# Attention units 4 to 9 scored in pairs, and the layer-2 matmuls dealt out anew, in a fused window-attention and feed-forward kernel

## The chip, the cores and the metric

The kernel runs on one core of one Trainium2 chip. The metric is the device time of one execution in microseconds (us). Three runs of the kernel before took 279.0 to 279.9 us, with a median of 279.62. Everything below that is said of a single instruction comes from one further execution of that kernel, taken by the hardware profiler.

## What is computed

Eight batches, eight heads, 576 tokens each and a head size of 64: attention in a band of 32 keys to either side, then a feed-forward network with one hidden layer over all 4608 tokens.

```python
scores = scale * np.matmul(q, k.transpose(0, 1, 3, 2))
mask = np.abs(pos[:, None] - pos[None, :]) <= window      # window = 32
scores = np.where(mask, scores, -1000000000.0)
attn = np.exp(scores - np.max(scores, axis=-1, keepdims=True))
attn = attn / (np.sum(attn, axis=-1, keepdims=True) + 1e-09)
x = np.matmul(attn, v).transpose(0, 2, 1, 3).reshape(B * S, H * D)   # 4608 x 512
h = x @ w_in                                                          # 512 x 2048
out = (h * (1.0 / (1.0 + np.exp(-1.702 * h)))) @ w_out                # 2048 x 512
```

## The kernel before

**Units and tiles.** The 4608 tokens are 36 units of 128 queries, and nine tiles of four units (512 tokens). A unit goes through `scores` (line 267: 24 small matmuls for q times k, then two exponentials on ScalarE), `band` (line 308: one multiplication by the mask on VectorE), `values` (line 316: 32 small matmuls with v) and `norm` (line 335: reciprocal and multiplication on VectorE). `x_T` and `x_T2` turn the result so that the features lie on the partitions. The first four units are scored in pairs (`scores_pair`, line 286): one pair takes 40 matmuls, the mask being added on TensorE by `seed` (line 261) ahead of the scores.

**Feed-forward.** Layer 1 of a tile (`l1_group`, line 512, called for n = 0 to 3) and layer 2 of half a tile (a pair of unit rows; `layer2`, line 597) are each split in 2 x 2 blocks and computed with seven products instead of eight; P1, P7, P6, P2, P5 or P4, P3 are the products. Tile 0 has plain layer 1 (`layer1_plain`, line 477), interleaved by hand with the first attention units in `opening` (line 662).

**The list of layer 2.** `layer2_plain(0, 0)` gives 32 closures with one matmul each, `layer2` gives 56 for every pair: eight for each product, in the order

```python
ps = [pair(*x) for x in pairs[:-1]] + [pair(*pairs[-1], end=(self.nc.sync, dve))]
out = ps[0][1] + ps[0][7]
for x, y in zip(ps, ps[1:]):
    out += x[6] + x[2] + x[4] + x[5] + y[1] + x[3] + y[7]
```

They stand in one list, `self.l2` (called `more` in `run`). `do(l2, n)` takes the next n of it and issues them; so the order on TensorE is written by hand, as numbers in the calls of `do`: in `opening`, in `first_layer1` (line 958, layer 1 of tile 1: four numbers for every n, used after P1, P7, P2 and P4 of layer 1), in `run` (line 895) and, from the third tile on, in `front` (line 820) and `back` (line 847, with the table `SHARES`). The list never learns where it is cut: which layer-2 matmul meets which cut depends on the sum of all numbers before.

**The banks of layer 2.** A pair has two banks of PSUM, LA and LB, each with two halves of 256 columns: a and c in LA, b and e in LB. P1 sums into a, and P7 into c. With P7's eighth matmul `after(7)` (lines 610 to 615) issues two copies, on the engine `seed2` (ScalarE at first, VectorE from line 944 on):

```python
self.copy(self.seed2, st["b"], st["a"])       # seed: P1's sum into bank LB
self.copy(self.seed2, st["s7"], st["c"])
```

P6 then goes on summing in b, on top of the copy. All engines work through their own instructions in order.

**Loads.** GpSimd issues the transfers of q, k, v (with a change of type) and of the weights, at first all together in `opening`, later by `LOADS` and by `fetch` in `first_layer1`; it also copies v with an offset of 64 tokens (`odd_v`, line 218). SyncE issues the transposing transfers and the stores.

Of the kernel before, what the change touches and what calls it, by code (L numbers as in the profile page):

```python
# [15 lines left out]
F32 = mybir.dt.float32  # L16
# [6 lines left out]
SQ = 64  # L23
# [3 lines left out]
class _Kernel:  # L27
# [7 lines left out]
    def __init__(self, ctx, tc, q, k, v, w_in, w_out, out):  # L35
        self.tc, self.nc = tc, tc.nc
        self.q, self.k, self.v, self.w_in, self.w_out, self.out = q, k, v, w_in, w_out, out
        self.B, self.H, self.S, self.D = q.shape
        self.N = self.B * self.S
        self.DM = self.H * self.D  # L40
        self.DFF = w_in.shape[1]
        self.scale = 1.0 / (self.D ** 0.5)
        self.NU = self.N // 128
        self.NT = self.N // TILE

        def pool(name, bufs, **kw):
# [5 lines left out]
        self.stage, self.kT, self.qT = {}, {}, {}  # L52
        self.p, self.acc, self.x, self.xT, self.xs = {}, {}, {}, {}, {}
        self.g, self.gs, self.o, self.sc = {}, {}, {}, {}
# [102 lines left out]
    def kq_tile(self, t):  # L157

        if ("T", t) not in self.stage:
            s = self.sb("gs", [128, 4, 576 + TILE], BF16, 2, "kq4")  # L160
            k, q = self.stage["T", t] = s[:, :, 0:576], s[:, :, 576:]
            for i in range(4):
                self.kT[4 * t + i] = k[:, :, 128 * i:128 * i + 128]
                self.qT[4 * t + i] = q[:, :, 128 * i:128 * i + 128]
            self.kT[4 * t + 4] = k[:, :, 512:576]
        return self.stage["T", t]
# [41 lines left out]
    def load_v(self, u, which=slice(None)):  # L208
# [21 lines left out]

    def place(self, c, u):
        t = self.sb(c + "T", [128, 4, 128], BF16, 7)
        (self.kT if c == "k" else self.qT)[u] = t
        return t
# [31 lines left out]

    def scores(self, u, tag):
        kT, q = self.kT[u], self.qT[u]
        nxt = self.k_first if u == self.NU - 1 else self.kT[u + 1][:, :, 0:64]
        sc = self.score_banks(tag)  # L270
        for hp in range(4):
            c = 128 * hp
            start = hp == 0
            for eo in range(2):
                r = slice(64 * eo, 64 * eo + 64)
                lo, hi = sc[eo][0:64], sc[eo][64:128]
                self.mm(lo[:, c:c + 64], kT[r, hp, 0:64], q[r, hp, 0:64], start=start)
                self.mm(hi[:, c:c + 128], kT[r, hp, 64:128], q[r, hp, :], start=start)
# [4 lines left out]
        for eo in range(2):  # L283
            self.nc.scalar.activation(p[:, eo].rearrange("k h s -> k (h s)"), sc[eo], AF.Exp, scale=self.scale)  # L284

    def scores_pair(self, u):
# [16 lines left out]
        for x in range(2):  # L303
            for eo in range(2):
                self.nc.scalar.activation(p[:, eo, x].rearrange("k h b s -> k (h b s)"), sc[2 * x + eo], AF.Exp,
                                          scale=self.scale)

    def band(self, u, eng=None):
# [3 lines left out]
        pv = p.rearrange("p e (h b) s -> p (e h) b s", b=2)  # L312
        msk = self.mask[:, a:b + 1:b - a, :].rearrange("p (o b) s -> p o b s", o=1)
# [40 lines left out]
    def values_four(self, u):  # L354
# [5 lines left out]
        for tag in self.FOUR:  # L360
            lo, n, pad = self.four(tag)
            for i in range(n):
                x, h = divmod(lo + i, self.H)
                at, more = pad + i * (D + 1), pad * (i == 0)
                for blk in range(2):
                    vt = (self.ve[(u + x) % 9], self.odd(u + x))[blk].rearrange("p h d -> p (h d)")
                    self.mm(self.acc[u][tag][64 * blk:64 * blk + 64, at - more:at + D + 1],
                            p[x][:, h % 2, h // 2 * 2 + blk, :], vt[:, h * (D + 2) - more:h * (D + 2) + D + 1],
                            start=(i == 0))
# [106 lines left out]

    def layer1_plain(self, t, f, half, tag, later=None, kept=None):

# [11 lines left out]
        if kept is not None:  # L490
            self.nc.vector.tensor_copy(kept, h)
            h = kept
# [169 lines left out]
    def opening(self):  # L662
# [18 lines left out]
        self.load_w1(256, 256)  # L681
        self.load_w1(512)
        for u in (0, 1):
# [7 lines left out]
        self.load_v(4, slice(1, 2))  # L691
        for u in (5, 6, 7, 8):
            self.load_v(u)
        for c in range(4):
            self.load_w2(c)
# [3 lines left out]
        self.seed(0, "AC")  # L699
        self.scores_pair(0)  # L700
        self.T_first("k", 1, ("LA", "LB"), (dve, dve))
        self.T_first("q", 1, ("B", "E"), (dve, act))
# [40 lines left out]
        act.activation(self.spark, self.spark, AF.Exp)  # L743
        gelus = []
        kept = [self.sb("s7", [128, 512], F32, 2)]
        room = self.sb("xs", [128, 2, 512], F32, 1, "room")
        kept += [room[:, i, :] for i in range(2)]
        h[:], n[0] = ["LA"], 0
        l1(1, 10, later=gelus, kept=kept[0])
        for i in (3, 1):  # L750
            self.w1_sums((i,), 1)
        for u in (4, 5, 6, 7):
            self.odd_v(u, pool)
        self.load_kq("k", 8)
        for u in (8, 9, 10, 11):
            self.fetch(u)
        h[:], n[0] = ["LB", "LA"], 0
# [8 lines left out]
        self.band(5)  # L766
        self.norm(4)
        h[:], n[0] = ["B", "E"], 0
        l1(None, 14, later=gelus)
        self.band(6)  # L770
        l1(None, 15, later=gelus)
        self.values(5, "t")
        self.norm(5)
        self.band(7)
        self.values(6, "AC")
        self.do(self.l2, 6)
        self.do(gelus)
        self.norm(6)
        self.values(7, "t")
        self.norm(7)  # L780
        self.do(self.l2, 2)
        self.w1_sums((2,), 1)
        self.g0_sum(0)
        self.x_T2(4, "A", act)
        self.do(self.l2, 4)
# [109 lines left out]
    def run(self):  # L895
        pool, act = self.nc.gpsimd, self.nc.scalar
        self.l2eng = self.seed2 = act
        more = self.l2 = self.layer2_plain(0, 0) + self.layer2([(i, j) for i in range(self.NT) for j in range(2)][1:-1],
# [17 lines left out]
        do(more, 4)  # L916
        self.values(8, "t")
        self.values(9, "AC")
        self.odd_v(12, pool)
        self.odd_v(13, pool)  # L920
        self.scores(11, "BE")
        self.norm(8)
        self.band(10)
        self.norm(9)
        do(more, 8)
        self.scores(12, "t")
        do(more, 4)
        self.values(10, "AC")
        self.norm(10)
        self.band(11)  # L930
        self.scores(13, "BE")
        do(more, 8)
        self.x_T2(8, "t", act)
        self.values(11, "AC")
        self.norm(11)
        self.scores(14, "BE")
        do(more, 4)
        self.x_T(10, "A", dve)
        do(more, 2)
        self.x_T(11, "C", dve)  # L940
        self.scores(15, "t")
        do(more, 2)
        do(self.x_sums(2))
        self.seed2 = dve
        self.odd_v(14, pool)
        self.odd_v(15, pool)
        self.ahead("kq", 16)
        late = self.back(2)
# [9 lines left out]
    def first_layer1(self):  # L958
# [7 lines left out]
        for n in range(4):  # L966
# [3 lines left out]
            self.odd_v(8 + n, self.nc.gpsimd)  # L970
            self.fetch(12 + n)
# [7 lines left out]
            self.l1_group(1, n, fill, lambda i: self.do(dv, 1))  # L979
            dv += self.g_sums(1, 2 * n, 2) + extra[n]  # L980
# [47 lines left out]
```

## Time and profile before

| of the kernel before | |
|---|---|
| three runs, median (lowest to highest) | 279.62 us (279.0 to 279.9) |
| the profiled execution, its own time | 279.59 us |
| span of its instructions | 277.8 us |
| TensorE busy | 266.3 us of the span, 3652 matmuls |
| VectorE, ScalarE, GpSimd busy | 212.1, 197.3, 138.6 us |
| packets of the transfers | 37.74 MB |

In the profile PE is TensorE's matmuls, PEld its weight loads, DVE VectorE, ACT ScalarE, POOL GpSimd and SP SyncE. L70 is the line that issues every matmul, L67 the line that issues every copy, so that such groups are told apart by the names of what they write and read: `o<-b,g` writes the tile o and reads b and g. Starts are microseconds from the span's beginning. Matmuls overlap in their pipeline: each lasts longer than the distance to the next.

### The profile page before, as it was taken

How to read it: one execution, taken by the hardware profiler on the slowest of the kernel's cores; microseconds unless marked ns; L12 is line 12 of the kernel's file. 1: busy time of each engine (PE TensorE's matmuls, PEld its weight loads, DVE VectorE, ACT ScalarE, POOL GpSimd, SP SyncE). 2: the span in 40 equal slices, each digit the busy share in tenths (PEclk: the TensorE clock that was granted, in tenths of full speed). 3: DMA queues.
4: the chain of work that ended last, by engine and by line, in shares of the span. 5: the costliest groups of instructions: out<-in, count | busy, mean ns of one | idle time of the engine just before them, and what ended most of it. 6: DMA issues, size and time to landing. Idle time of an engine off the chain costs nothing.

```text
span 277.8 us, 8904 instructions
## 1 busy us (share of the span) xinstructions
PE 266.3 (96%) x3652; PEld 224.8 (81%) x3652; DVE 212.1 (76%) x487; ACT 197.3 (71%) x346; POOL 138.6 (50%) x216
## 2 busy tenths in 40 slices
PE   1989999999999999999999999999999999999994
PEld 1668656888888888888888888888888888888883
DVE  3455898897899788878888887888798878855631
ACT  2586896989896689568966895698569856577420
POOL 8895597999592089729641974294430000000000
PEclk9999999999999999999999999999999999999999
DMA  8999999999999999999999999999992024202033
GB/s 86 166 206 195 178 207 168 170 150 164 139 162 189 155 121 153 174 176 166 188 178 153 130 172 148 163 145 139 136 136 77 2 82 74 76 2 76 2 113 117
DMA packets 150809, 37.74 MB, mean 136 GB/s; under 512 B 138608, under 2 KB 146416, under 8 KB 150768
## 3 DMA queue, kind: packets, MB, share of 16 engines
q0 software_dynamic: 106656, 18.42, 96.4%
q1 hardware_dynamic: 43664, 18.23, 38.0%
q8 instruction: 28, 0.46, 0.7%
q10 hardware_dynamic: 448, 0.52, 0.6%
q14 instruction: 13, 0.11, 0.1%
HBM read 36.83 MB, written 9.44 MB: 167 GB/s over the span
## 4 chain that ended last, share of the span: by engine, by line
PE 91%; DVE 4%; ACT 2%; issue 1%; POOL 1%; POOLq 0%; DVEq 0%
PE o L70 40%; PE h L70 39%; PE sc L70 5%; PE pv L70 4%; PE tp L179 1%; PE tp L203 1%; POOL kq L154 1%; ACT p L284 1%; DVE xn L345 1%; PE tp L409 0%; PE tp L249 0%; DVE b L433 0%; DVE o_sb L67 0%; PE tp L397 0%; ACT kq L67 0%
## 5 line engine op out<-in xcount | busy, mean ns | idle before, releaser
L524 ACT ACTIVATE g<-h 128x512 f16<-128x512 f32 x128 | 72.2, 599 | 37.9 <-PE h L70 31.6
L70 PEld LDWEIGHTS <-g 128*128 128x128 f16 x568 | 54.6, 98 | 8.1
L70 PE MATMUL h<-xs,a 128*128 128x256 f16 x384 | 57.6, 272 | 0.3 <-DVE h L537 0.3
L70 PEld LDWEIGHTS <-a 128*128 128x128 f16 x512 | 49.7, 97 | 8.8 <-issue 0.6
L70 PEld LDWEIGHTS <-w 128*128 128x128 f16 x496 | 47.6, 98 | 7.7
L70 PE MATMUL h<-xT,w 128*128 128x256 f16 (+1 forms) x368 | 53.6, 277 | 0.1
L70 PE MATMUL o<-w,g 128*128 128x256 f16 (+1 forms) x304 | 49.8, 284 | 0.0
L70 PEld LDWEIGHTS <-gs 128*128 128x128 f16 x416 | 39.7, 98 | 5.5 <-issue 0.2
L227 POOL COPY vo<-ve 64x264 int32<-64x264 int32 x71 | 35.1, 494 | 16.4 <-DMA ve<-in_v_dram 10.0
L70 PE MATMUL o<-b,gs 128*128 128x256 f16 x280 | 43.3, 273 | 0.0
L70 PE MATMUL o<-b,g 128*128 128x256 f16 x264 | 38.5, 273 | 0.0
L213 POOL DMA_DIRECT2D ve<-in_v_dram x40 | 34.1, 860 | 5.4 <-DMA w<-in_moe_w_out_dram 1.8
L537 DVE TENSOR_TENSOR h<-h,s 128x512 f32<-128x512 f32 x32 | 22.3, 698 | 18.3 <-PE h L70 18.2
L284 ACT ACTIVATE p<-sc 128x512 bf16<-128x512 f32 x64 | 32.6, 619 | 1.1 <-PE sc L70 1.0
L143 POOL DMA_DIRECT2D qst<-in_q_dram x35 | 28.2, 807 | 1.7 <-issue 1.6
L543 DVE TENSOR_TENSOR h<-h,s 128x512 f32<-128x512 f32 x32 | 22.3, 698 | 7.6 <-PE h L70 7.4
L143 POOL DMA_DIRECT2D kst<-in_k_dram x31 | 26.4, 854 | 0.6 <-DMA qst<-in_q_dram 0.4
L67 ACT COPY h<-h 128x512 f32<-128x512 f32 x32 | 18.8, 589 | 10.4 <-PE h L70 9.8
L886 POOL COPY seen<-gs 1x1 f16<-1x1 f16 x17 | 3.3, 196 | 39.3 <-DVE gs L456 39.3
L314 DVE TENSOR_TENSOR p<-p,mask 128x1024 bf16<-128x1024 bf16 x32 | 21.8, 699 | 0.7 <-ACT p L284 0.7
L67 ACT COPY o_sb<-o 128x256 f32<-128x256 f32 (+1 forms) x24 | 11.1, 462 | 12.8 <-PE o L70 12.8
L67 ACT COPY s<-h 128x512 f32<-128x512 f32 x32 | 19.2, 600 | 0.8
(94 smaller groups left out, 377.8 us busy)
## 6 DMA issues: line engine op xcount, KB each, us to landing
out_dram<-o_sb SPq DMA_DIRECT2D x33, 256.0 KB, 3.8
ve<-in_v_dram POOLq DMA_DIRECT2D x32, 128.0 KB, 6.3
kst<-in_k_dram POOLq DMA_DIRECT2D x25, 128.0 KB, 6.0
qst<-in_q_dram POOLq DMA_DIRECT2D x21, 128.0 KB, 5.7
w<-in_moe_w_out_dram POOLq DMA_DIRECT2D x4, 512.0 KB, 11.1
w<-in_moe_w_in_dram POOLq DMA_DIRECT2D x3, 512.0 KB, 9.3
qst<-in_q_dram POOLq DMA_DIRECT2D x7, 96.0 KB, 6.0
kq<-in_q_dram POOLq DMA_DIRECT2D x2, 256.0 KB, 6.0
```

What stands on the lines that cost most here:

```text
L67: (eng.copy if eng is self.nc.scalar else eng.tensor_copy)(out, in_)
L70: self.nc.tensor.matmul(out, lhsT, rhs, start=start, stop=stop, skip_group_check=True)
L143: self.nc.gpsimd.dma_start(t[off:off + n], src[b, :, s:s + n, :].rearrange("h s d -> s h d"))
L154: self.nc.gpsimd.dma_start(self.stage["first"][0:n // j, :, at:at + j], src[0, :, lo:lo + n, :].rearrange("h (p j) d -> p h j d", j=j))
L213: self.nc.gpsimd.dma_start(t[off:off + n, :, :self.D], self.v[b, :, s:s + n, :].rearrange("h s d -> s h d"))
L227: eng.tensor_copy(*((words(vo[64:128]), words(self.ve[u % 9][64:128])), (words(vo[0:64]), words(nxt)))[i])
L284: self.nc.scalar.activation(p[:, eo].rearrange("k h s -> k (h s)"), sc[eo], AF.Exp, scale=self.scale)
L314: (eng or self.nc.vector).tensor_mul(pv, pv, msk.to_broadcast([128, 8, 2, SQ]))
L524: act.activation(g[:, f, 256 * half:256 * half + 256], bank.rearrange("p (i n) -> p i n", i=2), AF.Gelu_apprx_sigmoid)
L537: dve.tensor_add(e, b, s7)
L543: dve.tensor_add(c, b, s7)
L886: self.nc.gpsimd.tensor_copy(self.seen, self.gs[t - (n == 0)][0:1, 2, c, 255:256])
```

## The change

1. **Pairs.** Units 4 and 5, 6 and 7, 8 and 9, 12 and 13 are scored together by the new `scores_two`: 40 matmuls for two units in place of 48, into four banks, with four exponentials as before. `band_two` masks units 4 to 9 by halves of heads (two multiplications for two units, as before), with three masks that `setup_pairs` lays out ahead by 12 small copies on VectorE. For this q of units 8 and 9, and of 12 and 13, lies in one tile (`place`).
2. **Opening.** Layer 1 of blocks 8 to 11 of tile 0 is done with 16 matmuls of 512 columns in place of 32 of 256; sums are parked in three single tiles; the table of the exponential is called up one block earlier; the activations of the parked blocks come in another order.
3. **Loads.** The third transfer of w_in goes in halves. Values 8 come in two halves (`load_half`), the second after the copies of v for units 4 to 7. Values 13 to 16 are asked for in n = 3 of `first_layer1` only, and q and k of unit 16 earlier in `run`.
4. **Sums of `first_layer1`** (VectorE) are dealt out by a new table, `sums`.
5. **Numbers of `do`.** In `first_layer1` n = 0 takes 1, 2, 3, 3 in place of 1, 1, 3, 3. The calls in `run` are cut anew, 64 in all as before; `opening` takes 18 as before, and so does each later n what it took. Scores 8 to 10 stand after the first 8 of `run`, and the second exponential of unit 10 after another 20.
6. **Banks.** Values 11 go to bank t (one reciprocal and one multiplication in place of two and two), x of units 8 and 9 is turned in bank A, x of 10 and 11 in one go in bank C.

```diff
+    def load_half(self, u, at):
+        b, s = divmod(128 * u + at, self.S)
+        self.nc.gpsimd.dma_start(self.ve[u % 9][at:at + 64, :, :self.D],
+                                 self.v[b, :, s:s + 64, :].rearrange("h s d -> s h d"))
...
+    def scores_two(self, u, tags):
+        k, q = [self.kT[u + i] for i in range(3)], self.qT[u]
+        sc = [x for tag in tags for x in self.score_banks(tag)]
+        for hp in range(4):
+            c = 256 * (hp % 2)
+            for eo in range(2):
+                r = slice(64 * eo, 64 * eo + 64)
+                for i in range(5):
+                    lo, hi = max(0, 64 * (i - 1)), min(256, 64 * (i + 1))
+                    rows = slice(64 * (i % 2), 64 * (i % 2) + 64)
+                    self.mm(sc[2 * (hp // 2) + eo][rows, c + lo:c + hi], k[i // 2][r, hp, rows], q[r, hp, lo:hi],
+                            start=c == 0 and i < 2)
...
+    def band_two(self, u):
+        m = self.masks[u].rearrange("p (e y) n -> p e y n", e=1, y=1).to_broadcast([128, 2, 2, 4 * SQ])
+        for x in range(2):
+            p = self.pair[u][:, :, x].rearrange("k e (y b) s -> k e y (b s)", y=2)
+            self.nc.vector.tensor_mul(p, p, m)
+
+    def setup_pairs(self):
...
+        for u in (4, 6, 8):
...
+                    self.nc.vector.tensor_copy(m[:, 0, at:at + SQ], self.mask[:, x, :])
...
-        self.load_w1(512)
+        self.load_w1(512, 256)
+        self.load_w1(768, 256)
...
-        l1(0, 8)
+        l1(None, 8)
...
-        l1(0, 10)
-        l1(1, 8)
+        l1(None, 9)
...
+        l1(None, 10, later=gelus, kept=kept[0])
+        act.activation(self.spark, self.spark, AF.Exp)
...
-        l1(1, 10, later=gelus, kept=kept[0])
+        l1(None, 11, later=gelus, kept=kept[1])
...
-        self.scores(4, "AC")
-        self.scores(5, "t")
-        l1(None, 12, later=gelus, kept=kept[1])
-        self.scores(6, "BE")
-        self.band(4)
-        l1(None, 13, later=gelus, kept=kept[2])
-        self.scores(7, "AC")
+        self.scores_two(4, ("AC", "t"))
+        copies, first = [], []
+        l1(None, 12, later=gelus, kept=kept[2], when=copies)
+        h[:] = ["LB"]
+        self.scores_two(6, ("BE", "AC"))
+        self.band_two(4)
+        l1(None, 13, later=first)
...
@@ run
-        self.l2eng = self.seed2 = act
+        self.l2eng, self.seed2 = self.nc.vector, act
...
-        self.scores(8, "t")
-        self.scores(9, "AC")
+        do(more, 8)
+        self.scores_two(8, ("t", "AC"))
+        exps = self.scores(10, "BE", True)
...
-        do(more, 20)
-        self.scores(10, "BE")
-        do(more, 12)
-        self.l2eng = dve
-        self.band(8)
-        self.band(9)
         do(more, 4)
+        self.band_two(8)
+        self.l2eng = act
+        do(more, 16)
+        do(exps)
+        do(more, 8)
         self.values(8, "t")
...
@@ first_layer1
+            chunks = ((1, 2, 3, 3), (1, 1, 3, 5), (2, 2, 8, 4), (2, 2, 6, 6))[n]
+            sums = ((0, 0, 1, 1, 2), (3, 1, 0, 1, 3), (1, 0, 2, 1, 2), (2, 1, 1, 0, 1))[n]
             def fill(i):
-                self.do(self.l2, dict(zip((1, 7, 2, 4), ((1, 1, 3, 3), (1, 1, 3, 5), (2, 2, 8, 4), (2, 2, 6, 6))[n]))[i])
-                self.do(dv, {1: 2, 7: 1, 2: 0, 4: 2}[i] if n else {1: 0, 7: 1, 2: 0, 4: 1}[i])
+                at = (1, 7, 2, 4).index(i)
+                self.do(self.l2, chunks[at])
+                self.do(dv, {1: sums[0], 7: sums[1], 2: 0, 4: sums[4]}[i])
```

Where the new numbers leave the cuts is best seen in the order of the instructions. On TensorE, in `front` of the fourth tile, the kernel before had P7 of a pair (it reads b3 and g), then the scores of two units (they read qT and kT), then P6 (it reads b2 and gs):

```order
L70 LDWEIGHTS g_2351
L70 MATMUL o_2742<-b3_78,g_2351 128x256
L70 LDWEIGHTS kT_2349
L70 MATMUL sc_2854<-qT_2435,kT_2349 64x64
L70 LDWEIGHTS kT_2349
L70 MATMUL sc_2854<-qT_2435,kT_2349 64x128
...
L70 LDWEIGHTS kT_2441
L70 MATMUL sc_2883<-qT_2439,kT_2441 64x64
L70 LDWEIGHTS gs_2422
L70 MATMUL o_2845<-b2_77,gs_2422 128x256
```

At the same place the changed kernel has:

```order
L71 LDWEIGHTS g_2315
L71 MATMUL o_2705<-b3_78,g_2315 128x256
L71 LDWEIGHTS gs_2386
L71 MATMUL o_2808<-b2_77,gs_2386 128x256
L71 LDWEIGHTS kT_2313
L71 MATMUL sc_2818<-qT_2399,kT_2313 64x64
L71 LDWEIGHTS kT_2313
L71 MATMUL sc_2818<-qT_2399,kT_2313 64x128
```

P6's first matmul has moved ahead of the 48 score matmuls, to the place right behind P7's eighth. The VectorE instructions there keep their order (the copy that seeds b is `o_2845<-o_2742` before and `o_2808<-o_2705` now):

```order
L67 COPY o_sb_2509<-o_2507 128x512
L67 COPY o_2845<-o_2742 128x256
L67 COPY s7o_2846<-o_2742 128x256
L455 TENSOR_TENSOR gs_2422<-gs_2422,g_2351 128x512
L456 TENSOR_TENSOR gs_2422<-g_2351,gs_2422 128x512
```

```order
L68 COPY o_sb_2472<-o_2470 128x512
L68 COPY o_2808<-o_2705 128x256
L68 COPY s7o_2809<-o_2705 128x256
L509 TENSOR_TENSOR gs_2386<-gs_2386,g_2315 128x512
L510 TENSOR_TENSOR gs_2386<-g_2315,gs_2386 128x512
```

Nothing moved on that engine. The second place is TensorE in `first_layer1` with n = 2, at the first pair of the list: before, eight matmuls of layer 1 (they write h) stood between P7 (`b3_78,gs_608`) and P6 (`b2_77,gs_608`):

```order
L70 LDWEIGHTS gs_608
L70 MATMUL o_1129<-b3_78,gs_608 128x256
L70 LDWEIGHTS a1_72
L70 MATMUL h_1151<-xs_983,a1_72 128x256
...
L70 LDWEIGHTS w1_70
L70 MATMUL h_1152<-xs_983,w1_70 128x256
L70 LDWEIGHTS gs_608
L70 MATMUL o_1209<-b2_77,gs_608 128x256
```

Now:

```order
L71 LDWEIGHTS gs_620
L71 MATMUL o_1112<-b3_78,gs_620 128x256
L71 LDWEIGHTS gs_620
L71 MATMUL o_1190<-b2_77,gs_620 128x256
L71 LDWEIGHTS a1_72
L71 MATMUL h_1135<-xs_969,a1_72 128x256
```

Again P6's first matmul follows P7's eighth, and the matmuls of layer 1 follow it. The third place is ScalarE in `run`, at the second pair, which still has its seed copied there (`o_1475<-o_1416` before, `o_1451<-o_1420` now; p is what an exponential writes):

```order
L67 COPY o_sb_1211<-o_1209 128x512
L67 COPY o_1475<-o_1416 128x256
L67 COPY s7o_1476<-o_1416 128x256
L284 ACTIVATE p_1451<-sc_1519 128x512
L284 ACTIVATE p_1451<-sc_1520 128x512
```

```order
L68 COPY o_sb_1192<-o_1190 128x512
L293 ACTIVATE p_1402<-sc_1377 128x512
L68 COPY o_1451<-o_1420 128x256
L68 COPY s7o_1452<-o_1420 128x256
L293 ACTIVATE p_1402<-sc_1500 128x512
```

One exponential, the one held back of unit 10, now stands between the store's copy and the seed. Over the whole list, P6's first matmul stands directly behind P7's eighth of the same pair at 15 places of 17 in the changed kernel and at none in the kernel before; at the two others, in the closing run of layer 2, matmuls of the other of the last two pairs lie between them in both kernels.

More of the change, by code (lines that the diff above doesn't have):

```diff
@@ L52, in __init__ @@
         self.stage, self.kT, self.qT = {}, {}, {}
+        self.pair = {}
         self.p, self.acc, self.x, self.xT, self.xs = {}, {}, {}, {}, {}
@@ L265, in seed, with scores @@
             self.mm(x, self.ident, self.bias, start=True)
-    def scores(self, u, tag):
+    def scores(self, u, tag, hold=False):
         kT, q = self.kT[u], self.qT[u]
@@ L306, in scores_pair @@
                                           scale=self.scale)
+    def scores_two(self, u, tags):
[10 more added lines that the diff above has]
+                            start=c == 0 and i < 2)
+        self.pp = self.sb("p", [128, 2, 2, 8, SQ], BF16, 2)
+        self.pair[u] = self.pp
+        p = self.pp.rearrange("k e x (y b) s -> k e x y b s", y=2)
+        for i in range(2):
+            self.p[u + i] = p[:, :, :, :, 2 * i:2 * i + 2, :]
+        for x in range(2):
+            for eo in range(2):
+                self.nc.scalar.activation(p[:, eo, x].rearrange("k y b s -> k (y b s)"), sc[2 * x + eo], AF.Exp,
+                                          scale=self.scale)
+    def band_two(self, u):
+        m = self.masks[u].rearrange("p (e y) n -> p e y n", e=1, y=1).to_broadcast([128, 2, 2, 4 * SQ])
+        for x in range(2):
+            p = self.pair[u][:, :, x].rearrange("k e (y b) s -> k e y (b s)", y=2)
+            self.nc.vector.tensor_mul(p, p, m)
+    def setup_pairs(self):
+        self.masks = {}
+        for u in (4, 6, 8):
+            m = self.cst.tile([128, 1, 4 * SQ], BF16, name=f"mask{u}")
+            self.masks[u] = m
+            for i in range(2):
+                cross = [(2 * (u + i) + j) % 9 == 8 for j in range(2)]
+                for j, x in enumerate((0 if cross[0] else 1, 2 if cross[1] else 3)):
+                    at = SQ * (2 * i + j)
+                    self.nc.vector.tensor_copy(m[:, 0, at:at + SQ], self.mask[:, x, :])
     def band(self, u, eng=None):
@@ L475, in g_tile, with layer1_plain @@
         return self.g[t]
-    def layer1_plain(self, t, f, half, tag, later=None, kept=None):
+    def layer1_plain(self, t, f, half, tag, later=None, kept=None, when=None):
         g = self.g_tile(t)
@@ L490, in layer1_plain @@
         if kept is not None:
-            self.nc.vector.tensor_copy(kept, h)
+            do = lambda h=h: self.nc.vector.tensor_copy(kept, h)
+            do() if when is None else when.append(do)
             h = kept
@@ L691, in opening @@
         self.load_v(4, slice(1, 2))
-        for u in (5, 6, 7, 8):
+        for u in (5, 6, 7):
             self.load_v(u)
+        self.load_half(8, 0)
         for c in range(4):
@@ L739, in opening @@
         self.g0_sum(7)
-        l1(0, 10)
-        l1(1, 8)
-        self.T_four("q", "tA", (dve, act))
[L743 to L747, printed above, removed]
+        l1(None, 9)
+        gelus = []
+        kept = [self.sb("s7", [128, 512], F32, 2) for i in range(2)]
+        kept.append(self.sb("xs", [128, 512], F32, 1, "room"))
+        l1(None, 10, later=gelus, kept=kept[0])
+        act.activation(self.spark, self.spark, AF.Exp)
+        self.T_four("q", "tA", (dve, act))
         h[:], n[0] = ["LA"], 0
-        l1(1, 10, later=gelus, kept=kept[0])
+        l1(None, 11, later=gelus, kept=kept[1])
         for i in (3, 1):
@@ L920, in run @@
         self.odd_v(13, pool)
+        self.ahead("kq", 16)
         self.scores(11, "BE")
@@ L924, in run @@
         self.norm(9)
-        do(more, 8)
-        self.scores(12, "t")
-        do(more, 4)
+        do(more, 12)
+        self.scores_two(12, ("t", "BE"))
         self.values(10, "AC")
+        self.band(11)
         self.norm(10)
[L930 to L934, printed above, removed]
+        do(more, 6)
+        self.values(11, "t")
         self.norm(11)
         self.scores(14, "BE")
+        self.x_T2(8, "A", act)
         do(more, 4)
-        self.x_T(10, "A", dve)
-        do(more, 2)
-        self.x_T(11, "C", dve)
+        self.x_T2(10, "C", dve)
         self.scores(15, "t")
-        do(more, 2)
+        do(more, 6)
         do(self.x_sums(2))
-        self.seed2 = dve
+        self.seed2 = self.l2eng = dve
         self.odd_v(14, pool)
         self.odd_v(15, pool)
-        self.ahead("kq", 16)
         late = self.back(2)
```

38 lines of the change are left out of this document (24 added, 14 removed).

## The prediction

> **What bounds the kernel now.** I read the page first: busy shares, the slices, and the shares of the chain that ended last.
>
> ```profile
> PE 266.3 (96%) x3652; PEld 224.8 (81%) x3652; DVE 212.1 (76%) x487; ACT 197.3 (71%) x346; POOL 138.6 (50%) x216
> PE   1989999999999999999999999999999999999994
> PEclk9999999999999999999999999999999999999999
> PE 91%; DVE 4%; ACT 2%; issue 1%; POOL 1%; POOLq 0%; DVEq 0%
> ```
>
> TensorE is busy for 266.3 of 277.8 us, at an undivided clock in all 40 slices, and it makes up 91% of the chain. Then I took stretches of the steady part, where one tile takes 27.4 us; the columns after the stretch's length are the busy time of PE, PEld, DVE, ACT and POOL, then the clock.
>
> ```profile
> 99.60:127.00 27.40, 27.40 (x385) 23.90 (x384) 23.17 (x54) 20.78 (x37) 19.18 (x32) 1.00 2.23 163
> 127.00:154.40 27.40, 27.40 (x385) 23.90 (x384) 23.05 (x54) 20.78 (x37) 15.41 (x26) 1.00 1.68 166
> 181.80:209.20 27.40, 27.40 (x386) 23.89 (x384) 23.06 (x53) 20.78 (x37) 14.66 (x27) 1.00 1.36 134
> ```
>
> TensorE does not stop at all there. So whatever holds it up is paid in full, and taking work off another engine brings nothing. Last I read the waits, and the durations of the two kinds of instruction that the change brings together.
>
> ```profile
> DVE o L67 <- PE o L70: 4.5, 12, 1.5
> PE h L70 <- DVE h L537: 0.3, 1, 0.3
> L70 PE MATMUL o<-b,g 128*128 128x256 f16 x264 | 38.5, 273 | 0.0
> L67 DVE COPY o<-o 128x256 f32<-128x256 f32 x15 | 6.5, 433 | 4.6 <-PE o L70 4.5
> L67 ACT COPY o<-o 128x256 f32<-128x256 f32 x2 | 0.8, 388 | 0.0
> ```
>
> The seed copy (`o<-o`) waits for TensorE 12 times; the other direction, P6 waiting for the seed copy, does not occur in the list of waits at all. That is the state that the change touches.
>
> **The large term: P6 right behind P7.** The seed copy starts when P7's eighth matmul is through, and P6's first matmul sums on top of it. The timeline of one place, in `front`:
>
> ```profile
> 128.97 1.04 PE L70 MATMUL o<-b,g 128*128 128x256 f16 x8
> 129.17 0.69 DVE L67 COPY o_sb<-o 128x512 f32<-128x512 f32 x1 [0.52 <-PE o L70]
> 129.94 0.70 PE L70 MATMUL sc<-qT,kT 64*64 64x64 bf16 x48
> 130.04 0.43 DVE L67 COPY o<-o 128x256 f32<-128x256 f32 x1 [0.18 <-PE o L70]
> 130.57 1.05 PE L70 MATMUL o<-b,gs 128*128 128x256 f16 x8
> ```
>
> P7's eight end at 128.97 + 1.04 = 130.01, the copy starts at 130.04 and ends at 130.47, P6 starts at 130.57. The 48 score matmuls between fill the copy's time almost to the point. P7's spacing is (1.04 - 0.273)/7 = 0.11 us, so its eighth starts at 129.74, and the next matmul could start at 129.85. In the changed kernel that next one is P6, which cannot start before the copy's end plus the way from VectorE to TensorE. For that way there is one row, the only matmul that waits for VectorE in the list above:
>
> ```profile
> 56.63 1.04 PE L70 MATMUL o<-b,gs 128*128 128x256 f16 x8
> 57.18 0.69 DVE L537 TENSOR_TENSOR h<-h,s 128x512 f32<-128x512 f32 x1
> 57.88 0.42 ACT L67 COPY o<-o 128x256 f32<-128x256 f32 x1
> 57.92 0.60 PE L70 MATMUL h<-xs,a 128*128 128x256 f16 x4 [0.25 <-DVE h L537]
> ```
>
> 57.18 + 0.69 = 57.87, and the matmul starts at 57.92: 0.05 us. So P6 starts at 130.52 instead of 129.85, a stall of **0.67 us**; the scores, queued behind P6 on TensorE, don't fill it. At the other kind of place, in `back`, the copy starts a little later after P7:
>
> ```profile
> 114.18 0.93 PE L70 MATMUL o<-b,g 128*128 128x256 f16 x7
> 115.21 0.43 DVE L67 COPY o<-o 128x256 f32<-128x256 f32 x1 [0.24 <-PE o L70]
> ```
>
> P7 ends at 115.11, the copy at 115.64, P6 could start at 115.69; P7's eighth starts at 114.84, the next slot is 114.95: **0.74 us**. Of the 15 places, 13 have their copy on VectorE: five in `front` (tiles 3 to 7) at 0.67 make 3.4 us, eight others at 0.74 make 5.9 us. Two have it on ScalarE. For the first, the rows of 56.63 to 57.92 hold: P7 ends at 57.67, the copy only at 57.88 + 0.42 = 58.30, since ScalarE is busy; P6 at 58.35 against 57.51 gives 0.84. The second:
>
> ```profile
> 69.63 1.04 PE L70 MATMUL o<-b,g 128*128 128x256 f16 x8
> 70.37 0.65 ACT L67 COPY o_sb<-o 128x512 f32<-128x512 f32 x1
> 71.05 0.36 ACT L67 COPY o<-o 128x256 f32<-128x256 f32 x1
> 71.61 1.05 PE L70 MATMUL o<-b,gs 128*128 128x256 f16 x8
> 72.58 0.45 PE L70 MATMUL sc<-qT,kT 64*64 64x64 bf16 x24
> 72.96 0.61 PE L70 MATMUL o<-w,g 128*128 128x256 f16 x4
> ```
>
> The copy ends at 71.41, P6 could start at 71.46 against 70.51: 0.95. There an exponential now goes ahead of the copy in place of other work; I leave 0.95 standing. Sum: 3.4 + 5.9 + 0.84 + 0.95 = **+11.1 us**. What is late next at each place is only what stood in front of P6 before, and it comes after P6 with its inputs long there.
>
> **What the change takes off TensorE.** Each change of tile shape costs: the eight of 71.61 take 72.58 - 71.61 = 0.97 us to the first score matmul, while 8 x 0.11 = 0.88: 0.09. The order has 71 runs of one shape instead of 76, so 5 x 0.09 = 0.45 less. Four pairs have 40 instead of 48 score matmuls over the same columns. The run of 24 takes 72.96 - 72.58 = 0.38, that of 48 took 130.57 - 129.94 = 0.63, so a matmul is worth 0.010, and 32 fewer bring between nothing (the columns decide) and 0.33 (the number does); I take 0.15. The 16 matmuls of 512 columns for 32 of 256 are the same work. Together **-0.6** (bounds -0.4 and -0.8).
>
> **Stalls in the opening.** A few short ones exist, as the 0.25 at 57.92, where layer 1 waited for VectorE; and the first score matmul of unit 4 starts late:
>
> ```profile
> 30.82 0.82 PE L70 MATMUL h<-xT,w 128*128 128x256 f16 x6
> 31.76 0.70 PE L70 MATMUL sc<-kq 64*64 64x64 bf16 x48
> ```
>
> Six matmuls take 0.66 and the change of shape 0.09, so 31.57 was due: 0.19, though the end of the six, at 31.64, lets only 0.12 of it appear as idle. In the two stretches from 18 to 72 us TensorE is idle for 0.28 and 0.25 us:
>
> ```profile
> 18.00:45.00 27.00, 26.72 (x404) 19.53 (x397) 20.79 (x42) 22.60 (x36) 19.71 (x27) 1.00 1.51 195
> 45.00:72.00 27.00, 26.75 (x356) 22.23 (x354) 22.51 (x45) 23.55 (x46) 23.71 (x34) 1.00 2.10 156
> ```
>
> With the part that such overlaps hide, I put the old stalls at 1.0. The changed order has its own: the scores of 4 still wait for the same copy of q (0.2), values 6 follow the second half of the mask of pair 6 more closely (0 to 0.35, by half of one multiplication of 699 ns), layer 1 with n = 1 waits for L537 behind sums dealt out anew (0 to 0.7, one L537), scores 14 take the bank of the last exponential of pair 12 (0 to 0.6, one exponential). I set these at 1.0 too, so **0**, with bounds -1.0 and +0.9.
>
> **Edits at about nothing.** The 12 mask copies stand on VectorE in front of the row of 12.03:
>
> ```profile
> 12.03 1.89 DVE L67 COPY kq<-tp 128x512 bf16<-128x512 bf16 x3 [2.28 <-PE tp L179]
> 11.08 0.75 POOL L127 DMA_DIRECT2D w<-in_moe_w_in_dram  x1 [0.24 <-DMA kq<-in_q_dram]
> L314 DVE TENSOR_TENSOR p<-p,mask 128x1024 bf16<-128x1024 bf16 x32 | 21.8, 699 | 0.7 <-ACT p L284 0.7
> ```
>
> VectorE is idle for 2.28 us there. No row has a copy of 64 columns; 12 copies at half of the seed copy's 0.43 would be 2.6, which leaves 0.3 over in the worst case. The load in halves adds one issue on GpSimd, 0.75, ahead of the copies of v and the next load; what waits for those is TensorE at values 0 (15 us) and the loads; even uncovered it is 0.75, and I take 0. The masks have the same two multiplications of 1024 elements for two units (699 ns). Values 8 in halves, values 13 to 16 later and the banks of units 8 to 11 act where VectorE and ScalarE wait for TensorE; one turned tile copied in one go saves an instruction there. The covers are TensorE's own rows.
>
> **Sum.** +11.1 - 0.6 + 0 = +10.5. The profiled execution took 279.59 us, 1.79 more than its span and 0.03 less than the median of the runs. 279.59 + 10.5 = 290.1 us.
>
> **A rule that speaks for more.** TensorE has idled before and kept its clock:
>
> ```profile
> 9.37 1.03 PE L70 MATMUL sc<-bias,ident 128*128 128x512 bf16 x2
> 10.33 1.08 PE L70 MATMUL sc<-kq 64*64 64x64 bf16 x40
> 16.20 0.40 PE L397 MATMUL tp<-identh,xn 128*128 128x128 f16 x4 [0.77 <-ACT p L305]
> 33.73 1.04 PE L70 MATMUL h<-xT,w 128*128 128x512 f16 x4
> ```
>
> After the idle 0.77 us at 16.2 no slice shows less than the full clock. Only the first matmuls are slow: two of 512 columns take 10.33 - 9.37 = 0.96, while four at 33.73 take 1.04. The Trainium skill, page "TensorE: Matmul & The Clock Gate", section "A second HAM failure mode: psum-queue depth-cycling", says that short idle times of TensorE between groups of matmuls can let its clock swing between half and full; by that rule fifteen new idle times would cost more than themselves. The trace so far does not agree (0.77 us idle, clock whole).
>
> **The rivals.**
> - *The seed is not late, and the kernel becomes faster* (0.05). Seed b needs only P1's sum, finished before P7 starts. If the copy in the changed kernel started by that, 0.7 us or more ahead of P7's eighth matmul, P6 would not wait and only the savings would be left: 279.59 - 0.6, with up to 0.7 of old stalls gone, 278.3. It decides at every place at once. Against it: copies start 0.03 to 0.10 after P7's last matmul, 12 times idle until then. This is also the case in which the new order doesn't do what it does on paper.
> - *Half of it is hidden* (0.06): the copy starts on time but the stall makes up for waits that I counted elsewhere, or the copy runs beside P7's last matmuls in the eight places of `back`. 279.59 + 3.4 + 1.8 - 0.6 = 284.2 up to 287.
> - *The copying engine is late as well* (0.07): the store's copy (0.69 at 129.17) runs until 129.86, 0.15 ahead of P7's end. Where an exponential or a sum of 0.4 to 0.7 stands in its way, a place costs 0.67 + 0.4 = 1.07; with ten places 4 us more: 294.
> - *The clock swings* (0.03): each stall is followed by matmuls at about half speed, for as long as the slow start of this trace seems to have lasted at the least (the rows of 9.37 to 11.4, some 2 us, and as much before): 3.2 us with half of it lost, 15 x 1.6 = 24 on top: 314. Against it stands the row of 16.20.
>
> **How the numbers follow.** Forecast 0.79, rivals 0.05, 0.06, 0.07 and 0.03. The bounds of the single terms add up to -2 and +2 around 290.1 (savings 0.2 each way, opening -1.0 and +0.9, the two ScalarE places 0.4 each, GpSimd and masks up to 1.0): 287.8 to 292.4, which leaves out about 2 in 10. A measurement of this kernel tells changes over 0.3%, 0.84 us. Faster by more than that 0.04, within it 0.01, slower 0.95.
>
> **What would show it.** In the changed kernel's waits: PE o waiting for DVE o, 13 times 0.6 to 0.8 us, about 9 in all, and twice for ACT o; one tile of the steady part takes 27.4 + 0.67 + 0.74 = 28.8 us, TensorE's busy time in it unchanged; the run of scores starts behind P6's first matmul. The first step is wrong if P6 starts within 0.2 us after P7's eighth; the second if the span outside of these waits changes by more than 1.5 us; the clock rival if PEclk shows less than 9 after 20 us.

## The result, and the profile after

| | kernel before | changed kernel |
|---|---|---|
| median of five runs (lowest to highest) | 279.45 us (279.0 to 279.9) | 290.61 us (290.4 to 290.95) |
| ratio, 95% interval | 1 | 1.0402 (1.0385 to 1.0419) |
| profiled execution, span | 279.59, 277.8 us | 290.95, 289.2 us |

The change costs 11.2 us, within the range and 0.5 us above the value forecast. Medians, ranges and ratios here and below leave out four runs that lie over 1.5% above the fastest of their kernel, one of experiment 1 (690.92 us), one of 9 (282.88) and two of 10 (283.69 and 1517.55). The page of the changed kernel: span, busy shares, clock by slice, and the chain by engine.

```profile
span 289.2 us, 8807 instructions
PE 266.7 (92%) x3604; PEld 222.2 (77%) x3604; DVE 215.8 (75%) x497; ACT 196.6 (68%) x345; POOL 138.5 (48%) x218
PEclk9999999999999999999999999999999999999999
PE 77%; DMA 8%; DVE 5%; ACT 4%; POOL 3%; issue 1%; SPq 0%; DVEq 0%; POOLq 0%
```

TensorE is about as busy as before (266.7 us against 266.3) in a span longer by 11.4 us: the work did not grow, the gaps did. The groups and the waits say which (the columns of a wait: us in total, times, the longest):

```profile
L71 PE MATMUL o<-b,gs 128*128 128x256 f16 x280 | 44.1, 273 | 9.3 <-DVE o L68 7.5 <-ACT o L68 1.8
PE o L71 <- DVE o L68: 7.5, 13, 0.7
PE o L71 <- ACT o L68: 1.8, 2, 1.0
```

The group that holds P6 had no idle time ahead of it; now it has 9.3 us, 13 times behind VectorE's seed copy and twice behind ScalarE's. These 9.3 us count only what lies behind the modelled end of P7's last matmul. From start to start each wait is longer by 0.273 - 0.11 = 0.16, 15 times 2.4, which makes 11.7. One place of the kind in `front`, on the timeline:

```profile
133.28 1.04 PE L71 MATMUL o<-b,g 128*128 128x256 f16 x8
133.48 0.69 DVE L68 COPY o_sb<-o 128x512 f32<-128x512 f32 x1 [0.34 <-PE o L71]
134.35 0.43 DVE L68 COPY o<-o 128x256 f32<-128x256 f32 x1 [0.18 <-PE o L71]
134.84 0.27 PE L71 MATMUL o<-b,gs 128*128 128x256 f16 x1 [0.52 <-DVE o L68]
135.04 0.70 PE L71 MATMUL sc<-qT,kT 64*64 64x64 bf16 x48
```

P7 ends at 134.32, the copy starts at 134.35 and ends at 134.78, and P6's first matmul starts at 134.84; the 48 scores, which covered this time before, stand behind it. In `back`:

```profile
117.85 0.82 PE L71 MATMUL o<-b,g 128*128 128x256 f16 x6
118.78 0.43 DVE L68 COPY o<-o 128x256 f32<-128x256 f32 x1
119.26 0.27 PE L71 MATMUL o<-b,gs 128*128 128x256 f16 x1 [0.59 <-DVE o L68]
```

The copy starts 0.11 us after P7's end (118.67) here. The stretch of one tile, and the next:

```profile
105.50:134.35 28.85, 27.74 (x384) 23.95 (x384) 23.65 (x52) 20.83 (x37) 19.97 (x33) 1.00 1.59 159
134.35:163.15 28.80, 27.68 (x384) 23.95 (x384) 23.17 (x52) 20.92 (x37) 15.00 (x26) 1.00 1.66 152
```

28.8 us instead of 27.4, of which TensorE stands idle for 1.1, and the clock is whole.

### The profile page after: what moved, and what is told of

Same layout as the page of the kernel before. It is cut to its first block, busy times and chain, and to the rows that moved or that the text cites. A ratio compares the mean times of both kernels' runs of the same rounds, so it can differ in the third digit from the quotient of the medians.

```text
span 289.2 us, 8807 instructions
## 1 busy us (share of the span) xinstructions
PE 266.7 (92%) x3604; PEld 222.2 (77%) x3604; DVE 215.8 (75%) x497; ACT 196.6 (68%) x345; POOL 138.5 (48%) x218
## 4 chain that ended last, share of the span: by engine, by line
PE 77%; DMA 8%; DVE 5%; ACT 4%; POOL 3%; issue 1%; SPq 0%; DVEq 0%; POOLq 0%
PE o L71 36%; PE h L71 33%; DMA o_sb<-in_k_dram 3%; PE sc L71 3%; PE pv L71 3%; DMA qT<-qst 2%; DMA ve<-in_v_dram 2%; DVE o L68 2%; POOL kq L155 1%; POOL ve L214 1%; ACT p L340 1%; DVE p L347 1%; PE tp L259 1%; DVE h L598 1%; ACT kq L68 1%
## 5 line engine op out<-in xcount | busy, mean ns | idle before, releaser
L71 PEld LDWEIGHTS <-w 128*128 128x128 f16 x480 | 45.9, 98 | 9.4 <-issue 0.8
L71 PE MATMUL o<-b,gs 128*128 128x256 f16 x280 | 44.1, 273 | 9.3 <-DVE o L68 7.5
L233 POOL COPY vo<-ve 64x264 int32<-64x264 int32 x71 | 34.0, 479 | 18.6 <-DMA ve<-in_v_dram 15.2
L71 PE MATMUL o<-b,g 128*128 128x256 f16 x264 | 39.6, 273 | 0.0
L592 DVE TENSOR_TENSOR h<-h,s 128x512 f32<-128x512 f32 x32 | 22.4, 699 | 18.1 <-PE h L71 17.7
L214 POOL DMA_DIRECT2D ve<-in_v_dram x39 | 33.2, 865 | 2.5 <-DMA w<-in_moe_w_in_dram 1.2
L68 ACT COPY h<-h 128x512 f32<-128x512 f32 x32 | 18.2, 570 | 12.5 <-PE h L71 11.0
L293 ACT ACTIVATE p<-sc 128x512 bf16<-128x512 f32 x48 | 25.2, 605 | 1.3 <-PE sc L71 1.3
L68 ACT COPY o_sb<-o 128x256 f32<-128x256 f32 (+1 forms) x24 | 11.1, 462 | 12.4 <-PE o L71 12.4
L71 PE MATMUL h<-xT,a 128*128 128x256 f16 x128 | 19.2, 272 | 0.1
```

The lines of the kernel that those rows point to most:

```text
L68: (eng.copy if eng is self.nc.scalar else eng.tensor_copy)(out, in_)
L71: self.nc.tensor.matmul(out, lhsT, rhs, start=start, stop=stop, skip_group_check=True)
L233: eng.tensor_copy(*((words(vo[64:128]), words(self.ve[u % 9][64:128])), (words(vo[0:64]), words(nxt)))[i])
L293: exps = [lambda eo=eo: self.nc.scalar.activation(p[:, eo].rearrange("k h s -> k (h s)"), sc[eo], AF.Exp, scale=self.scale) for eo in rang ...
L592: dve.tensor_add(e, b, s7)
```

## The experiments

The theory: P6's first matmul directly behind P7's eighth waits for the seed copy, at 15 places. The main rival: the loss lies in the other edits (pairs, loads, sums), or in scores and values that come late because the list of layer 2 runs ahead. Ratios are against the kernel before on the same chip, with 95% intervals.

**1. The changed kernel without the shift.**

```diff
-            chunks = ((1, 2, 3, 3), (1, 1, 3, 5), (2, 2, 8, 4), (2, 2, 6, 6))[n]
+            chunks = ((1, 1, 3, 3), (1, 1, 3, 5), (2, 2, 8, 4), (2, 2, 6, 6))[n]
```

> The changed kernel with the four numbers of n = 0 back at 1, 1, 3, 3: all later layer-2 matmuls are one further back, and P6's first matmul again has scores, values or layer 1 between itself and P7's eighth; every other edit stays. Theory (P6 waits for the seed copy): the 15 waits go, 11.7 us by the profile of the changed kernel, so about 279 us. Rival (the other edits cost the time: pairs, loads, sums): it stays above 285 us.

Measured: 280.73 us, 1.0043 (1.0018 to 1.0068). One number takes back ten of the eleven microseconds, and no wait of P6 is left in the profile. But the time is 1.2 us above the kernel before (0.0043 x 279.4), not at it, and it scatters from 279.05 to 282.4 us. The timeline of this profile shows a wait that neither kernel had, at the scores of unit 15:

```profile
76.43 0.24 PE L71 MATMUL sc<-qT,kT 64*64 64x64 bf16 x2
78.07 0.44 PE L71 MATMUL sc<-qT,kT 64*64 64x64 bf16 x22 [1.40 <-DMA kT<-kst]
```

They wait 1.4 us for the turned k of unit 16. So the other edits are not all free once the big loss is gone; experiments 5, 6 and 9 to 12 look for the reason.

**2. The shift alone, in the kernel before.** The same table's first row, in the old code, from 1, 1, 3, 3 to 1, 2, 3, 3.

> The kernel before with only the numbers of n = 0 changed, to 1, 2, 3, 3. Theory: the same 15 waits appear, 5 at 0.69, 8 at 0.75 and 2 of about 1 us, 11.4 us together, so 290.5 to 291. Rival (other edits cost the time): within 1 us of the kernel before.

Measured: 290.75 us, 1.0409 (1.0391 to 1.0427): the whole loss, without any other edit. Its waits are those of the changed kernel:

```profile
PE o L70 <- DVE o L67: 7.5, 13, 0.7
PE o L70 <- ACT o L67: 1.5, 2, 0.8
```

The rival that the other edits cost the time falls with this.

**3. The shift the other way.** n = 0 at 1, 0, 3, 3 in the kernel before: P7's eighth matmul now stands behind the cut, with P6.

> The kernel before with n = 0 at 1, 0, 3, 3: one layer-2 matmul fewer ahead of everything later, so that P7's eighth matmul moves behind the cut and stands directly ahead of P6 again, while scores and values come earlier than before. Theory (it is the two standing side by side): 5 places in front at 0.69, 2 late ones at 0.75, 6 with four matmuls of layer 1 between at 0.3, 2 on ScalarE near 0.95, together 8.7, so about 288 us. Rival (the scores and values come late when the list runs ahead): no loss, 279 to 280 us.

Measured: 295.96 us, 1.0594 (1.0573 to 1.0614). The sign is the theory's: the list runs behind, scores come early, and it is slower still. The size is not, 16.6 us in place of 8.7. The timeline of a place in `back`, which I had put at 0.3:

```profile
121.32 0.28 PE L70 MATMUL o<-b,g 128*128 128x256 f16 x1
121.52 0.61 PE L70 MATMUL h<-xT,w 128*128 128x256 f16 x4
121.59 0.42 DVE L380 TENSOR_TENSOR xn<-pv,rec 128x256 f16<-128x256 f32 x1
121.93 0.20 DVE L379 RECIPROCAL rec<-pv 128x7 f32<-128x7 f32 x1
122.16 0.62 DVE L380 TENSOR_TENSOR xn<-pv,rec 128x448 f16<-128x448 f32 x1
122.70 0.42 DVE L67 COPY o<-o 128x256 f32<-128x256 f32 x1
123.18 0.38 PE L70 MATMUL o<-b,gs 128*128 128x256 f16 x2 [1.04 <-DVE o L67]
```

P7's eighth ends at 121.60, but the seed copy, now issued behind the values, stands behind three instructions of their normalisation in VectorE's order (L380, L379, L380) and starts at 122.70. All six places of this kind wait 1.04 or 1.05 us, and from start to start the 15 waits of this profile add up to 15.7 us. The price of such a wait is P7's end plus the copy plus all that the copying engine has queued ahead of it. I had counted only the first two.

**4. The seed as the second of the two copies, in the changed kernel.**

```diff
-                    self.copy(self.seed2, st["b"], st["a"])
                     self.copy(self.seed2, st["s7"], st["c"])
+                    self.copy(self.seed2, st["b"], st["a"])
```

> The changed kernel with the two copies behind P7 in the other order: s7 first, then the seed that P6 waits for. Theory: each of the 15 waits grows by the distance of two such copies, 0.34 to 0.43 us, 5 to 6 us in all, so 295.7 to 297 us. Rival (the wait is for P7 itself or for the bank, not for the copy): no change, 290.6 us.

Measured: 294.77 us, 1.0549 (1.0529 to 1.0568), 4.1 us more than the changed kernel (0.0147 x 279.4), less than the 5 to 6 expected.

```profile
135.27 0.42 DVE L68 COPY s7o<-o 128x256 f32<-128x256 f32 x1 [0.18 <-PE o L71]
135.61 0.42 DVE L68 COPY o<-o 128x256 f32<-128x256 f32 x1
136.09 0.28 PE L71 MATMUL o<-b,gs 128*128 128x256 f16 x1 [0.86 <-DVE o L68]
```

The wait follows the copy: 0.86 instead of 0.52 in `front`, 0.34 more, as the two copies start 0.34 apart. It grew less in `back`, from 0.59 to 0.85, since the first of the two copies no longer starts 0.11 but 0.03 after P7 there. That P6 waits for P7 or for the bank is out.

**7. The same swap in the kernel before.**

> The kernel before with s7 copied ahead of the seed. Theory (in the kernel before the work between P7 and P6 covers the copy almost to the point): the five places with 48 scores have 0.05 us to spare and lose about 0.3 each, the two late ones 0.12 to spare and lose 0.2 each, one of the two on ScalarE loses 0.2, the places with values lose nothing; 279.4 + 2.1 = 281.5 us. Rival (the copy has ample room): no change.

Measured: 282.0 us, 1.0094 (1.008 to 1.0108), 2.7 us more, against 2.1 expected; the profiled span grew by 1.9.

```profile
PEld L70 <- DVE o L67: 1.7, 5, 0.3
PE o L70 <- DVE o L67: 1.1, 5, 0.2
```

Five places lose up to 0.3 each, as expected: the kernel before has 48 scores in them and 0.05 us to spare. The losses of 0.2 expected at three other places do not show in the list of waits, and where the rest of the 2.7 us lies is open.

**8. The shift for the first two places only.** In `run` of the changed kernel, the last `do(more, 6)` becomes `do(more, 5)`.

> The changed kernel with one layer-2 matmul fewer at the end of run (5 in place of 6), so that only the first two places, whose seed ScalarE copies, keep P6 right behind P7, and the 13 later ones do not. Theory (the places add up one by one): 13 waits fewer, 0.86 + 5 x 0.69 + 7 x 0.755 = 9.6 us, so 281.0 us. Rival (the first two delays shift everything after them, or the steady waits are hidden by others): above 283 us or below 280 us.

Measured: 281.5 us, 1.0085 (1.0071 to 1.01). Nine of eleven microseconds are gone, and the only wait of this kind left is ScalarE's:

```profile
PE o L71 <- ACT o L68: 1.8, 2, 1.0
```

So the places count one by one, and the early ones don't set the late ones.

**5 and 6. What is left at the old cuts: the loads.** Experiment 5 is the first one with values 13 to 16 asked for as before; 6 undoes the other load edits as well.

```diff
-            self.ahead("kq", 12 + n)
-            for u in ((), (), (), (13, 14, 15, 16))[n]:
-                self.load_v(u)
+            self.fetch(12 + n)
```

> The changed kernel with n = 0 at 1, 1, 3, 3 as in the first experiment, and with values 13 to 16 asked for along with q and k as before, not all four after n = 3. Theory (their burst delays the last turned tile of k, for which the scores of unit 15 waited 1.6 us): that wait goes, the scatter from 279.0 to 282.4 us narrows, and the time is 279.0 to 279.3 us. Rival (another load or the pairs cost it): 280.5 us and as scattered as the first experiment.

> As the one before, with all other load edits undone too: w_in's third transfer whole, values 8 whole, q and k of unit 16 asked for late. Only the pairs, sums, banks and numbers of the change are left. Theory (the loads are hidden but for values 13 to 16): the same as the one before, within 0.4 us, near 279.0. Rival (the halves free something or hold something up in the opening, where the copies of v were waited for 0.44 us): apart by 0.5 us or more.

Measured: 280.92 us, 1.0062 (1.0044 to 1.008), and 279.5 us, 1.0004 (0.999 to 1.0018). The theory of the burst falls: with values 13 to 16 back, the wait is there still, for q of unit 15 as well:

```profile
PE sc L71 <- DMA qT<-qst: 1.6, 1, 1.6
PE sc L71 <- DMA kT<-kst: 0.8, 2, 0.5
```

With all loads as before, it is gone, and so is the loss. So the load edits together cost about 1.1 us at the old cuts (1.0043 against 1.0004), and what is left (pairs, sums, banks and the new opening) brings nothing that the time shows: in the profile of 6 TensorE is busy for 264.5 us instead of 266.3, but waits 1.0 us for w_in in the opening, a wait that the profile of the kernel before does not have.

**9 and 10. Which of the loads.** 9 keeps only the halves of w_in and of values 8; 10 undoes only the early q and k of unit 16.

> n = 0 at 1, 1, 3, 3; values 13 to 16 asked for as before and q and k of unit 16 late as before, but the halves of w_in's third transfer and of values 8 kept. Theory (anything issued between 68 and 75 us, be it the burst of values or q and k of unit 16, delays the turning of q 15 and k 16, and the halves are harmless): no wait at 75 to 79 us, and 278.3 to 279.2 us. Rival (the halves cost it): 280.5 us or more.

> n = 0 at 1, 1, 3, 3; only q and k of unit 16 late as before, the burst of values 13 to 16 kept after n = 3. Theory (either of the two moved loads is enough to delay the turning of k 16): still a wait of about 1.5 us at 78 us, and 280.3 to 281 us. Rival (it was q and k of unit 16 alone): 279.2 us or less.

Measured: 279.89 us, 1.0023 (0.9996 to 1.0051), from 278.56 to 282.3, and 280.62 us, 1.0039 (1.0019 to 1.0059). The first lies between theory and rival. The second has the time that was expected, but the profile of that execution shows no wait at 78 us, and another in its place, for the x of a later tile:

```profile
PE h L71 <- DVE xs L495: 1.2, 1, 1.2
```

This does not settle which load it is. What the profiles of 1, 5 and 10 share is that turned tiles (transposing transfers) land late, now one, now another, while the kernel with all loads back stays between 279.06 and 280.27 us.

**11 and 12. A faster version.** 11 is 9 with `do(more, 4)` ahead of the scores of unit 14; 12 is 11 with the exponential's table called up behind the copies of q in the opening.

> As the kernel with the halves kept, with four layer-2 matmuls moved ahead of the scores of unit 14, which had waited 0.40 us for the last exponential of pair 12 in every kernel with the new order. Theory (TensorE is the bound, each wait of its own is paid in full): 0.3 to 0.4 us less than that kernel, 278.0 to 278.8 us. Rival (the turned k 16 or a later wait takes it back): the same within 0.1 us.

> As the one before, with the exponential's table called up behind the copies of the turned q of tile 1 again, as in the kernel before. The scores of unit 4 waited 0.28 us for ScalarE's copy. Theory (the copy comes 1.3 us sooner, but the first exponentials now come behind the table): the 0.28 goes and 0 to 0.5 comes back at values 4, so between 0.3 us faster and 0.3 us slower than the one before. Rival (the table was what made the copy late, and the exponentials have room): 0.28 us faster.

Measured: 280.21 us, 1.0036 (1.0015 to 1.0058), and 279.52 us, 1.0003 (0.9991 to 1.0015). In 11 unit 14's wait for the exponential is gone, and a wait for turned k of 0.84 us stands in its place, with another of 1.09 after it: the gain was taken back, as the rival said. 12 takes 0.7 us less than 11 (the intervals just touch), more than either expectation of it, and its runs lie between 279.1 and 280.11 us, as close together as those of 6, though it keeps the halves of 9. So the spread does not hang on the loads alone, and why 12 does better was not found. None of the versions is faster than the kernel before by more than the measurement can tell; the best single execution, 278.56 us with 9, had none of the waits for turned k and q in its profile.

## Why the prediction was right, point by point

- **P6 behind P7** (+11.1 forecast): the step held, by 2 and 8 above all. From start to start the waits are 0.69 (five in `front`), 0.755 (seven), 0.86 (the first on VectorE), 0.95 and 1.19 (ScalarE), together 11.7. The two on ScalarE were put at 0.84 and 0.95. At the second, the exponential that the order shows ahead of the seed was left unpriced:

```profile
70.22 1.04 PE L71 MATMUL o<-b,g 128*128 128x256 f16 x8
70.82 0.63 ACT L68 COPY o_sb<-o 128x512 f32<-128x512 f32 x1
71.29 0.67 ACT L293 ACTIVATE p<-sc 128x512 bf16<-128x512 f32 x1
71.78 0.46 ACT L68 COPY o<-o 128x256 f32<-128x256 f32 x1
72.29 0.27 PE L71 MATMUL o<-b,gs 128*128 128x256 f16 x1 [1.02 <-ACT o L68]
```

  P7 ends at 71.26, the copy starts at 71.78, because the exponential of 0.67 runs first.
- **Savings and the opening** (-0.6 and 0): the span grew by 11.4, so all that is not P6 brought -0.3 in place of -0.6. Of the waits that I had listed, unit 14's scores behind the exponential (0.24) and unit 4's behind ScalarE's copy (0.21) are there; those of values 6 and of layer 1 with n = 1 are not. One for k in the opening was not on the list, nor was a later one of layer 1 behind L592:

```profile
26.59 0.61 PE L204 MATMUL tp<-ident,o_sb 128*64 128x128 bf16 x14 [0.45 <-DMA o_sb<-in_k_dram]
77.53 0.41 PE L71 MATMUL sc<-qT,kT 64*64 64x64 bf16 x21 [0.24 <-ACT p L340]
95.47 0.60 PE L71 MATMUL h<-xs,a 128*128 128x256 f16 x4 [0.24 <-DVE h L592]
```


  A wait of the first values of tile 1 for their mask (0.35 at 38.15) was not on it either, and the wait at 95.47 comes long after the n = 1 for which layer 1 was listed. The -0.3 splits into two larger terms. TensorE's busy time in the changed kernel holds the ends of P7's last matmuls (the 2.4 us above), over which the next matmul ran before; without them it is 264.3, 2.0 less than before. Its idle time outside P6's waits is 289.2 - 266.7 - 9.3 = 13.2 us against 277.8 - 266.3 = 11.5, so 1.7 more. This is an estimate, since ends are modelled: experiment 2, with the work of the kernel before, comes out 1.0 lower by the same reckoning. So the savings were 1 to 2 us, not 0.6, and the new waits cost more than the old by about as much, not 0. That the two nearly cancel is luck, not foresight.
- **Loads at about nothing**: right for the changed kernel, wrong as a statement on the loads. There the cover was not TensorE's work but the delay at the first P6 places, which let the turned tiles land in time. With P6 off the path (1, 5), the waits for them appear. Experiment 8 fits this: it has the loads of 1 and the delays of the first two places only, and its profile shows no wait for turned tiles. That the delay is what hid them is still my reading of single profiles.
- **The rivals**: that the seed needs only P1's sum and is not late was wrong: its copy waited for P7's end at each place. The clock rival did not happen in the changed kernel, with 15 idle times of 0.5 to 1.0 us some 14 us apart, but see below. Its price of 1.6 us for a swing does not follow from the rows it names (2 us and as much before make 4, half of it 2.0), though the swing of experiment 11 cost about 1.7.
- **Total**: 290.1 forecast, 290.61 measured. The bounds of the terms, added as listed, give -2.0 and +2.9, not -2 and +2; the measured time lies inside either way.

## What to carry to other kernels

Where work of one kind is dealt out from a list by counts, one count early in the program decides what stands between a producer and its consumer at every later cut: look, in the order, at what lies between the two, and add up whether it covers the other engine's way. Price such a wait as producer's end, plus the copy, plus everything queued ahead of the copy on its engine. A load that is "hidden anyway" is hidden by the present schedule: after a gain elsewhere it may be the next thing to wait for.

## What the runs showed of the hardware that was not expected

In experiment 11 the profiled execution shows TensorE at half its clock in the middle of the kernel. The windows after the two waits for turned k (the column ahead of the last two is the granted clock), and the rows around them:

```profile
74.00:78.40 4.40, 2.47 (x58) 1.77 (x51) 2.60 (x8) 2.74 (x5) 3.97 (x6) 1.00 0.73 92
78.40:80.20 1.80, 1.80 (x29) 1.37 (x30) 1.08 (x3) 1.08 (x2) 1.80 (x3) 0.54 1.77 264
80.20:82.00 1.80, 1.80 (x11) 1.26 (x10) 0.00 (x0) 0.57 (x1) 1.80 (x3) 0.51 2.16 163
82.00:86.00 4.00, 4.00 (x37) 3.48 (x36) 3.19 (x6) 3.50 (x6) 0.16 (x1) 1.00 2.77 124
```

```profile
75.67 0.44 PE L71 MATMUL sc<-qT,kT 64*64 64x64 bf16 x22 [0.84 <-DMA kT<-kst]
76.04 1.07 PE L463 MATMUL tp<-identh,xn 128*128 128x128 f16 x16
78.37 0.53 PE L71 MATMUL sc<-qT,kT 64*64 64x64 bf16 x22 [1.09 <-DMA kT<-kst]
80.08 1.06 PE L71 MATMUL h<-xT,w 128*128 128x256 f16 x4
```

After 1.93 us idle within 4.4 us the clock was 0.54 and 0.51 in two windows of 1.80 us: four matmuls of 256 columns take 1.06 us from 80.08, where four take 0.60 at the full clock (95.47 above). What is missing to the full clock is (0.46 + 0.49) x 1.80 = 1.7 us, as 3.4 us at half clock would cost. This execution (282.29 us) was the slowest of its twelve.

That the two waits set it off is not shown. In experiment 5 TensorE was idle for longer in less time, 2.07 us of 4.0, and the clock stayed whole:

```profile
76.00:78.00 2.00, 0.92 (x13) 0.71 (x10) 1.01 (x2) 1.47 (x3) 2.00 (x4) 1.00 1.43 124
78.00:80.00 2.00, 1.01 (x28) 0.80 (x29) 1.29 (x4) 0.27 (x1) 2.00 (x3) 1.00 1.50 282
```

A single wait of 1.40 us (experiment 1) and the 15 of the changed kernel left it at 1.00 as well. The mean granted clock was 0.993 in this execution, 0.994 in one run each of experiments 1, 5 and 10 and in two of 9 (282.0 to 283.7 us), and at least 0.997 in every other run; 0.006 of 280 us is 1.7 us. So a swing of this size seems to make up the upper end of their scatter, but no profile shows those runs.

It looks like the swing that the Trainium skill describes in "TensorE: Matmul & The Clock Gate", sections "HAM oscillation — how this bites in real kernels" and "A second HAM failure mode: psum-queue depth-cycling". The first of them gives idle times of TensorE above about 3.4 us as what to avoid; here the two idle times ahead of it were 0.84 and 1.09 us, so this trace fits the second better, which speaks of short idle times and gives no limit, while one of 1.6 us in experiment 5 left the clock whole.
